# Another written engine order for the units of a gated linear attention in front of a mixture of experts

## The chip, the cores and the metric

The kernel runs on one core of a Trainium2 chip. A core has five engines that run their own instruction streams and meet only at semaphores: PE (TensorE, matmuls into PSUM), DVE (VectorE), ACT (ScalarE), POOL (GpSimd) and SP (which here only issues DMAs). The metric is the device time of one execution in microseconds (us); less is better. A difference of 2% (8 us) is about what a comparison of such runs is taken to show.

## The reference

Two stages follow each other. The first is a recurrent attention over 768 time steps for 4 batches and 8 heads of width 40, the second sends each of the 3072 tokens (rows of 320 numbers) through one of 16 experts.

```
m_new  = max(f[t] + m, i[t])
f_stab = exp(f[t] + m - m_new);  i_stab = exp(i[t] - m_new);  m = m_new
C = f_stab * C + i_stab * outer(v[t], k[t]);   n = f_stab * n + i_stab * k[t]
y[t] = sigmoid(o[t]) * (C @ q[t]) / max(|n . q[t]|, 1)
# x = y as 3072 rows of 320
group  = argmax(x @ w_group);  expert = argmax(x @ w_expert[group])
out[row] = softmax weight of group * softmax weight of expert
           * (relu(x[row] @ w1[expert]) @ w2[expert])
```

## The kernel before, in words

**Units.** The recurrence is cut into chunks of 128 steps. One *unit* is one chunk of one batch with its 8 heads; there are 6 x 4 = 24 units, u = 0 to 23, with chunk c = u // 4 and batch b = u % 4. A unit needs, in the order of the data:

- `decays(u, half)`: for four heads, four matmuls that spread a row of gate sums `Z` over the partitions (L186, into a PSUM tile `sp`), and four exponentials on ACT (L188) into the decay tile `ab`. `upper` (L166, POOL) then zeroes the future half of `ab`.
- `scores(u)` (L197): eight matmuls of keys and queries, 40 rows deep in a 64-row tile, into two more `sp` tiles; `masked` (L202, DVE) multiplies them with `ab` into `pt`.
- `keyw` (L209, POOL) weighs the keys, `state` (L248, PE) makes the new part of the carried matrix, `decayed` (L255, POOL) and `state2` (L266, or L268 in the first chunk, DVE) bring the carried matrix `Cflat` up to date.
- `carried` (L228, PE) multiplies the queries with the carried matrix, `carried2` (L238, DVE) scales the result in PSUM, and `values` (L277, PE) adds `pt` times the values to it.
- `norm1`, `norm2`, `gated` (L283 to L293, DVE), `rows` (L298, POOL) make the finished rows x; `gate` (L163, ACT) is the tanh of the output gate. `store_rows` copies a piece (L305, ACT) and sends x to DRAM; `turn_rows` transposes x (L316, PE) and copies it to SBUF (L318, L319, ACT).

**Routing.** After each chunk `logits` (L341, PE) and the generator `route` (some 18 short DVE steps, one group of small matmuls L385 to L397, one exponential L366) find each token's expert and its place in that expert's list. The steps are "chores", taken a few at a time by `go_on(n)`. `mark` (DVE L472 and L475, POOL L483) and `listing` (L490, PE) build the lists, `listed` (L496, DVE) adds them up. In unit 21 `select` and `load_x` gather the first expert's rows by two indirect DMAs issued by POOL (L593).

**Gates.** `gate_sums` (scans and subtractions on DVE), `parts` (splits the sums into three bf16 rows of `Z`, ACT and DVE in turn), `gate_ends`, `gate_cols` and `gate_scales` make what decays and carried need. Chunk 0 comes first, chunk 1 next, and chunks 2 to 5 together as 512-wide operations.

**What sets the order.** All of this stands under a manual schedule: each engine runs its instructions in the order in which the code calls the stages. Units 1 to 21 come from `unit(u)`, which mixes stages of units u-1, u, u+1 and u+2; units 22 and 23 from `last_units`. The PSUM tiles `sp` are three buffers in turn, and a unit takes four of them. `STEPS` says how many routing steps are taken at the three places of a unit. The experts behind it (L679 to L878) are not touched.

Of the kernel before, what the change touches and what calls it, by code (L numbers as in the profile page):

```python
# [66 lines left out]
def lstm_moe(ctx: ExitStack, tc: tile.TileContext, gates, qkT, nat, wcat, w1, w2, cst, out):  # L67
# [284 lines left out]
    def route(c, bank, lv):  # L352
# [595 lines left out]
    def unit(u):  # L948
        one, two, three = STEPS.get(u) or ((2, 2, 1), (0, 0, 0), (2, 2, 2), (2, 2, 2))[u % B]
        run(load_qk, u + 3)  # L950
        norm1(u - 1)
# [12 lines left out]
        if u + 2 < NU:
            decays(u + 2, 0)
        scores(u + 1)
        if u == NU - 3:
            cast()
        if u % B == 1 and u > B:
            logits()  # L970
        decayed(u)
        if u == 2:
            turn_rows(0)
        rows(u - 1)
        values(u)
        if u + 2 < NU:
            decays(u + 2, 1)
        run(state2, u)
        go_on(two)
        if u == NU - 3:  # L980
            rt["early"] = select(top[:, 0, :], nc.vector)
            xgs[0] = load_x(EARLY, rt["early"], True)
        masked(u + 1, 0)
        masked(u + 1, 1)
        if u == NU - 3:
            do(lows, 1)
        store_rows(u - 1)
        if u == 6:
            first_rows()
        if u > 1:  # L990
            run(keyw, u + 1)
        if u + 2 < NU:
            upper(st_[u + 2]["ab"], 0.0)
        gate(u + 1)
# [427 lines left out]
```

## Time and profile before

| | us |
|---|---|
| median of 3 runs | 399.84 (395.16 to 401.24) |
| profiled execution, its own time | 399.05 |
| its span, first to last instruction | 397.5 |
| PE busy | 363.9 (92%) |
| DVE busy | 315.0 (79%) |
| ACT busy | 255.5 (64%) |
| POOL busy | 158.2 (40%) |

The units take the first 155 us or so, the experts the rest. Among the experts PE is busy nearly all the time; among the units it is not, and the granted clock falls below full in the slices between 20 and 60 us. A unit is recognised in the trace by its group of 16 score matmul records (L197; a matmul of 32-bit numbers leaves two records); the times of these groups are used below as unit marks: scores of unit 2 run from 20.11 us, of unit 6 from 51.75, of unit 7 from 58.63, of 11 from 79.93, of 15 from 101.28, of 19 from 123.41, of 20 from 130.44, of 22 from 140.83 and of 23 from 145.57.

### The profile page before, as it was taken

The numbers are of one execution on the slowest core, as the hardware profiler recorded it, in microseconds if no ns is written. First come the engines' busy times: TensorE is split into PE (matmuls) and PEld (weight loads), VectorE is DVE, ScalarE is ACT, GpSimd is POOL, SyncE is SP. The second block draws the span as 40 slices with busy tenths as digits, with TensorE's granted clock in tenths as the row PEclk, the third lists the DMA queues.
The fourth block names the chain that finished last, engine by engine and source line by source line (L and its number), as shares of the span: only waits on it lengthen the run. The fifth ranks groups of instructions, "written<-read, shape, count | busy, mean of one in ns | idle before, by whom it ended". The sixth has DMA issues, their size and how long they took to land.

```text
span 397.5 us, 10540 instructions
## 1 busy us (share of the span) xinstructions
PE 363.9 (92%) x3993; PEld 331.0 (83%) x3993; DVE 315.0 (79%) x787; ACT 255.5 (64%) x624; POOL 158.2 (40%) x186
## 2 busy tenths in 40 slices
PE   8578598989897998899999999999999999999994
PEld 5467477777776776778999999999999998999993
DVE  3778548888899988547889879878979879899892
ACT  3556545657674674364578566758768768788792
POOL 6266316767755560041532262152243124242221
PEclk9969679999999999899999999999999999999999
DMA  7645326686655699025976585774975786579100
GB/s 202 208 132 170 116 70 188 210 286 193 186 194 156 207 365 350 12 69 189 350 248 255 199 335 181 280 266 157 318 283 181 257 330 222 203 267 327 36 16 16
DMA packets 18886, 81.79 MB, mean 206 GB/s; under 512 B 3248, under 2 KB 7062, under 8 KB 15250
## 3 DMA queue, kind: packets, MB, share of 16 engines
q1 hardware_dynamic: 15010, 68.35, 50.7%
q0 software_dynamic: 3600, 12.39, 8.7%
q8 instruction: 32, 0.52, 0.6%
q10 hardware_dynamic: 224, 0.36, 0.4%
q14 instruction: 20, 0.16, 0.1%
HBM read 71.65 MB, written 9.93 MB: 205 GB/s over the span
## 4 chain that ended last, share of the span: by engine, by line
PE 51%; DVE 15%; issue 15%; POOL 9%; ACT 5%; DMA 2%; POOLq 1%; SPq 0%; ACTq 0%; DVEq 0%
PE psh L767 18%; PE po L817 5%; PE po L819 4%; PE po L818 4%; PE po L695 3%; DVE pt L202 2%; PE acc L277 2%; POOL x L298 2%; PE sp L197 2%; POOL ab L166 2%; POOL kw L209 2%; PE psh L792 2%; PE po L823 1%; POOL out_dram L597 1%; DVE w2l L738 1%
## 5 line engine op out<-in xcount | busy, mean ns | idle before, releaser
L597 POOL DMA_INDIRECT out_dram<-y,ix x32 | 36.8, 1150 | 113.3 <-ACT y L831 85.0
L188 ACT ACTIVATE ab<-sp,bcol 128x128 f32<-128x128 f32 x176 | 50.1, 368 | 27.6 <-PE sp L186 19.7
L767 PE MATMUL psh<-xhl,w1h 128*128 128x256 f32 (+4 forms) x336 | 57.9, 303 | 0.2
L817 PE MATMUL po<-w2h,hh 128*128 128x320 f32 (+1 forms) x176 | 55.6, 316 | 0.0
L819 PE MATMUL po<-w2h,hh 128*128 128x320 f32 (+1 forms) x176 | 54.3, 309 | 0.0
L818 PE MATMUL po<-w2l,hh 128*128 128x320 f32 (+1 forms) x176 | 54.3, 309 | 0.0
L738 DVE TENSOR_TENSOR w2l<-w2s,w2h 128x640 fp32r<-128x640 f32 x60 | 47.8, 823 | 6.4 <-ACT w2h L734 5.7
L767 PEld LDWEIGHTS psh<-xhl,w1h 128*128 128x128 f32 x336 | 49.3, 188 | 2.1 <-DVE xhl L800 0.6
L767 PE MATMUL psh<-xhl,wsk 128*128 128x256 f32 (+4 forms) x168 | 47.5, 322 | 0.0
L767 PE MATMUL psh<-xhl,w1l 128*128 128x128 f32 (+6 forms) x256 | 47.5, 267 | 0.0
L593 POOL DMA_INDIRECT xg<-x_d,ix x32 | 35.8, 1117 | 27.3 <-PE psh L792 7.8
L166 POOL TENSOR_SCALAR_AFFINE_SELECT ab<-ab 128x1024 f32<-128x1024 f32 (+1 forms) x26 | 27.0, 1037 | 48.8 <-ACT ab L188 45.4
L738 DVE TENSOR_TENSOR w1l<-w1s,w1h 128x1024 fp32r<-128x1024 f32 x32 | 39.1, 1222 | 4.2 <-ACT w1h L734 3.9
L767 PEld LDWEIGHTS psh<-xhl,w1l 128*128 128x128 f32 x256 | 42.1, 188 | 0.4
L734 ACT CAST w2h<-w2s 128x640 fp32r<-128x640 f32 x60 | 41.5, 725 | 0.0
L277 PE MATMUL acc<-nt,pt 128*64 128x64 f32 x768 | 30.1, 236 | 6.5 <-DVE acc L238 6.1
L277 PEld LDWEIGHTS acc<-nt,pt 128*64 128x64 f32 x768 | 26.7, 149 | 10.9 <-DVE acc L238 8.3
L734 ACT CAST w1h<-w1s 128x1024 fp32r<-128x1024 f32 x32 | 33.4, 1045 | 0.0
L817 PEld LDWEIGHTS po<-w2h,hh 128*128 128x128 f32 (+1 forms) x176 | 32.6, 185 | 0.3
L819 PEld LDWEIGHTS po<-w2h,hh 128*128 128x128 f32 (+1 forms) x176 | 32.6, 185 | 0.2 <-DVE hh L869 0.2
L818 PEld LDWEIGHTS po<-w2l,hh 128*128 128x128 f32 (+1 forms) x176 | 32.6, 185 | 0.0
L202 DVE TENSOR_TENSOR pt<-sp,ab 128x512 f32<-128x512 f32 x48 | 30.8, 682 | 1.8 <-PE sp L197 1.3
(207 smaller groups left out, 810.6 us busy)
## 6 DMA issues: line engine op xcount, KB each, us to landing
w1s<-in_w_dram SPq DMA_DIRECT2D x12, 1536.0 KB
w2s<-in_w_dram SPq DMA_DIRECT2D x14, 1280.0 KB
nt<-in_nat_dram SPq DMA_DIRECT2D x24, 484.0 KB
qk<-in_qkT_dram SPq DMA_DIRECT2D x48, 160.0 KB
x_d<-x SPq DMA_DIRECT2D x24, 192.0 KB
w1s<-in_w_dram SPq DMA_DIRECT2D x4, 768.0 KB
w1s<-in_w_dram POOLq DMA_DIRECT2D x2, 1536.0 KB, 8.5
w2s<-in_w_dram SPq DMA_DIRECT2D x4, 640.0 KB
```

The lines of the kernel that those rows point to most:

```text
L166: nc.gpsimd.affine_select(out=a, in_=a, pattern=[[0, a.shape[1]], [1, P]], compare_op=ALU.is_ge, fill=fill, base=0, channel_multiplier=-1)
L188: nc.scalar.activation(ab[:, 4 * hh + pr, :], t[:, pr, :], AF.Exp, bias=bcol[:, c, at[pr]:at[pr] + 1])
L202: nc.vector.tensor_tensor(pt, t["pm"][hh], t["ab"][:, 4 * hh:4 * hh + 4, :], op=ALU.mult)
L277: mm(acc[r, j, :], t["pm"][j % 2][:, j // 2, r], nt[:, j * D1:j * D1 + WIN], start=(c == 0 and n == 0), stop=(n == H - 1), skip_group_chec ...
L593: return nc.gpsimd.indirect_dma_start(out=o, out_offset=None, in_=src, in_offset=bass.IndirectOffsetOnAxis(ap=idx, axis=0))
L597: return nc.gpsimd.indirect_dma_start(out=out, out_offset=bass.IndirectOffsetOnAxis(ap=idx, axis=0), in_=y, in_offset=None, bounds_check=N ...
L734: nc.scalar.copy(t[names[0]][:, dst], src[r][:, s])
L738: nc.vector.tensor_tensor(o, src[r][rows, s], h.bitcast(F32), op=ALU.subtract)
L767: mm(ps[:, g, 0:n_], w[:, s], x, start=(part == 0 and n == 0), stop=(part == 1 and n == len(todo[1]) - 1), skip_group_check=True)
L817: mm(po[0:m], hh[:, f, t], w2h[:, s], start=st0, stop=False)
L818: mm(po[0:m], hh[:, f, t], w2l[:, s], start=False, stop=False)
L819: mm(po[0:m], hh[:, f, tl], w2h[:, s], start=False, stop=sp0)
```

## The change

Nothing is computed differently but for the shape of the score matmuls and the place of three small routing results. What moves:

- In `unit(u)` the order becomes: first half of `decays(u+2)`, `carried2(u)`, `decayed(u)`, `scores(u+1)`, the norms of u-1, second half of `decays(u+2)`, `state2(u)`, `keyw(u+1)`, `rows(u-1)`, `values(u)`, `masked(u+1)`, lists, logits, routing steps, `store_rows` and `turn_rows` of u-1, `gate(u+1)`, `state(u+1)`, `carried(u+1)`, `upper(u+2)`, and last the gate steps and marks. Routing steps now stand in one place behind the masks, with a second number for units 18 to 20.
- Unit 0 is now a call of `unit` too. The separate products `spread` for units 0 and 1 (L1182) are gone: these units use `decays` as the others do, which needs `parts(0, P)` first. The rest of the gate work is cut into steps that stand at the ends of units 0 to 5.
- `scores` splits each matmul in two halves of 64 columns: 16 matmuls in 64x64 tiles, four different tiles in turn, for 8 in 64x128.
- Of the routing, `m2` and `oh5` go to PSUM, and one copy (`ohg`) is added per chunk.
- `gate_cols` takes its PSUM tile from the `sp` buffers.

```
 def scores(u):
-                mm(t["pm"][hh][:, pr, :], qk[r, 0, pr, :], qk[r, 1, pr, :], start=True, stop=True)
+                for o in HALVES:
+                    mm(t["pm"][hh][o, pr, :], qk[r, 0, pr, o], qk[r, 1, pr, :], start=True, stop=True, skip_group_check=True)
...
-        m2 = post.tile([P, n * 5], F32, name="m2")
+        m2 = bank[:, LT - P + n * 26:LT - P + n * 31]
...
-        oh5 = post.tile([P, n, 5, 4], F32, name="oh5")
+        oh5 = bank[:, LT + P:LT + P + n * 20].rearrange("p (b g e) -> p b g e", b=n, g=5)
...
+        ohg = post.tile([P, n, 4], F32, name="ohg")
+        nc.vector.tensor_copy(ohg, oh5[:, :, 0, :])
...
+    STEPS = {18: (6, 3), 19: (9, 0), 20: (0, 0)}
...
     def unit(u):
+        n = STEPS.get(u) or ((5, 0), (0, 0), (6, 0), (7, 0))[u % B]
         run(load_qk, u + 3)
+        if u + 2 < NU:
+            decays(u + 2, 0)
+        carried2(u)
+        decayed(u)
+        scores(u + 1)
+        if u:
+            norm1(u - 1)
+            norm2(u - 1)
+            gated(u - 1)
         run(load_nt, u + 3)
+        if u == NU - 3:
+            listed()
+            rt["early"] = select(top[:, 0, :], nc.vector)
+            xgs[0] = load_x(EARLY, rt["early"], True)
+        if u + 2 < NU:
+            decays(u + 2, 1)
+        if u == NU - 3:
+            cast()
+        run(state2, u)
+        keyw(u + 1)
+        if u:
+            rows(u - 1)
+        values(u)
+        masked(u + 1, 0)
+        masked(u + 1, 1)
+        listed()
...
+        if u % B == 1 and u > B:
+            logits()
+        go_on(n[0])
+        if u:
+            store_rows(u - 1)
+            turn_rows(u - 1)
+        gate(u + 1)
+        run(state, u + 1)
+        carried(u + 1)
+        if u + 2 < NU:
+            upper(st_[u + 2]["ab"], 0.0)
+        for x in gate_steps.pop(u, ()):
+            x()
+        go_on(n[1])
+        if u % B == 1 and u > B:
+            chores.append(turned_logits(u // B - 1))
+        if u % B in (1, 3) and B < u < NU - 4:
+            mark()
         if u == NU - 4:
+            listed()
             mark()
             mark()
             fill_up()
+            listing(ps_1.tile([P, 4, P], F32, name="tp", tag="tp"))
...
     def last_units():
         c, d = NU - 2, NU - 1
+        carried2(c)
+        scores(d)
         norm1(c - 1)
         norm2(c - 1)
         gated(c - 1)
-        carried2(c)
-        scores(d)
...
     def parts(lo, hi):
+        nc.scalar.copy(Z[0:n, lo:hi], a)
+        yield
         nc.vector.tensor_tensor(r, a, Z[0:n, lo:hi], op=ALU.subtract)
         yield
+        nc.scalar.copy(m, r)
         nc.scalar.copy(Z[n:2 * n, lo:hi], m)
+        yield
         nc.vector.tensor_tensor(r, r, m, op=ALU.subtract)
         yield
+        nc.scalar.copy(Z[2 * n:3 * n, lo:hi], r)
         yield
...
     def gate_cols(cl, ch):
-        tp = ps_1.tile([P, 8, 64], F32, name="tp", tag="tp" if ch < NCH else "lg")
+        tp = ps_s.tile([P, 8, 64], F32, name="tp", tag="sp")
...
-        steps(first, 5)
+        steps(first, 4)
+        early = parts(0, P)
+        steps(early)
+        steps(first)
+        gate_cols(0, 1)
+        steps(early, 4)
...
-        spread(0, 0)
-        spread(0, 1)
+        decays(0, 0)
         scores(0)
+        decays(0, 1)
...
+        decays(1, 0)
+        steps(early, 2)
         masked(0, 1)
+        state(0)
+        decays(1, 1)
+        steps(early, 3)
...
+        far2 = parts(2 * P, S)
+        one, two = (lambda: steps(far)), (lambda: steps(far2))
+        gate_steps.update({0: [near_scales, one], 1: [lambda: gate_ends(1, 2), one, one], 2: [one], 3: [one, two],
+                           4: [two, two], 5: [two, two, far_scales]})
+        for u in range(6):
             unit(u)
```

On PE, in one unit of the steady stretch (u = 9; `sp` is the decay or score tile, `st` the new state, `acc` the output, `tp` the transposed rows, each L186 pair stands four times), the order before, from the first decay half of unit 11 on:

```order
L186 LDWEIGHTS ind_b
L186 MATMUL sp<-Z,ind_b 128x128
...
L197 MATMUL sp<-qk_107 128x128 x8
L341 MATMUL lg<-xT,wc 32x128 x12
L277 MATMUL acc<-nt_114,pt 64x64 x16
L186 LDWEIGHTS ind_b
L186 MATMUL sp<-Z,ind_b 128x128
...
L248 MATMUL st<-nt_115,kw 40x41 x8
L228 MATMUL acc<-Cflat,qk_107 64x2x41 x8
L347 MATMUL lg<-cs,lgT 128x128
```

The same unit with the change:

```order
L186 LDWEIGHTS ind_b
L186 MATMUL sp<-Z,ind_b 128x128
...
L198 MATMUL sp<-qk_107 64x128 x16
L186 LDWEIGHTS ind_b
L186 MATMUL sp<-Z,ind_b 128x128
...
L278 MATMUL acc<-nt_114,pt 64x64 x16
L342 MATMUL lg<-xT,wc 32x128 x12
L317 MATMUL tp<-cs,x 128x128 x2
L317 MATMUL tp<-cs,x 64x128
L249 MATMUL st<-nt_115,kw 40x41 x8
L229 MATMUL acc<-Cflat,qk_107 64x2x41 x8
L348 MATMUL lg<-cs,lgT 128x128
```

The second decay half moved from behind the values to right behind the scores, and the transposes of the rows from the unit's end to right behind the values.

On POOL, from unit 19 to unit 21 (`x` are finished rows, `ab` the masked decays, `mark` the list products, `xg` the gathered rows), the order before:

```order
L166 AFFINE_SELECT ab_110<-ab_110 128x1024
L483 TENSOR_TENSOR mark<-mark,iw 128x2x48 x4
L298 TENSOR_TENSOR x<-sr,den 128x320
L166 AFFINE_SELECT ab_111<-ab_111 128x1024
L298 TENSOR_TENSOR x<-sr,den 128x320
L593 DMA xg<-x_d,ix 128x384 x2
L166 AFFINE_SELECT ab_112<-ab_112 128x1024
```

And with the change:

```order
L166 AFFINE_SELECT ab_110<-ab_110 128x1024
L485 TENSOR_TENSOR mark<-mark,iw 128x2x48 x2
L299 TENSOR_TENSOR x<-sr,den 128x320
L166 AFFINE_SELECT ab_111<-ab_111 128x1024
L485 TENSOR_TENSOR mark<-mark,iw 128x2x48 x4
L595 DMA xg<-x_d,ix 128x384 x2
L299 TENSOR_TENSOR x<-sr,den 128x320
L166 AFFINE_SELECT ab_112<-ab_112 128x1024
```

The four mark products of unit 20 now stand behind the rows and the mask of that unit, and the rows of unit 20 behind the two gathers.

## Rows read from the trace of the kernel before

**Rows 1.** Busy time by stretch: start:end, length, then PE, PEld, DVE, ACT, POOL, granted clock

```profile
20.11:51.75 31.64, 23.45 (x340) 19.76 (x341) 21.36 (x46) 17.10 (x59) 16.15 (x17) 0.72 0.48 147
51.75:58.63 6.88, 6.88 (x117) 5.47 (x116) 3.70 (x15) 3.25 (x13) 0.51 (x1) 0.73 0.01 2
58.63:79.93 21.30, 19.00 (x407) 16.35 (x405) 17.49 (x62) 13.52 (x51) 15.32 (x26) 1.00 0.66 202
79.93:101.28 21.35, 19.41 (x410) 16.77 (x408) 18.51 (x64) 13.63 (x51) 13.99 (x21) 1.00 0.72 224
101.28:123.41 22.13, 19.42 (x410) 16.77 (x409) 19.93 (x69) 13.50 (x51) 13.97 (x21) 1.00 0.60 186
```

**Rows 2.** Waits by engine and line, 60 to 165 us: total us, times, longest

```profile
PE lg L385 <- DVE oh L380: 5.1, 5, 1.7
PE acc L277 <- DVE acc L238: 3.3, 4, 1.8
PE st L248 <- POOL kw L209: 2.7, 5, 1.5
```

**Rows 3.** Timeline of PE in one unit: start, us, operation, records, [idle before]

```profile
90.34 0.39 PE L186 MATMUL sp<-Z,ind_b 96*128 96x128 bf16 x4
90.66 1.16 PE L197 MATMUL sp<-qk 64*128 64x128 f32 x16
91.75 1.15 PE L277 MATMUL acc<-nt,pt 128*64 128x64 f32 x32
92.83 0.40 PE L186 MATMUL sp<-Z,ind_b 96*128 96x128 bf16 x4
93.55 0.51 PE L248 MATMUL st<-nt,kw 128*40 128x41 f32 x16 [0.32 <-POOL kw L209]
```

**Rows 4.** Timeline of PE and ACT: a decay half and its exponentials on an idle ACT

```profile
88.60 0.40 PE L186 MATMUL sp<-Z,ind_b 96*128 96x128 bf16 x4
...
89.10 1.14 ACT L188 ACTIVATE ab<-sp,bcol 128x128 f32<-128x128 f32 x4 [1.08 <-PE sp L186]
```

**Rows 5.** Timeline of PE: 128-column matmuls in one tile, and in four tiles in turn

```profile
5.41 1.15 PE L1182 MATMUL wide<-A__129,cs 32*128 32x128 f32 x8
...
96.37 1.00 PE L341 MATMUL lg<-xT,wc 128*32 128x128 f32 x24
```

**Rows 6.** Timeline, 42 to 52 us: PE at the lower clock, the last gate chain

```profile
42.91 1.98 PE L277 MATMUL acc<-nt,pt 128*64 128x64 f32 x32 [2.87 <-DVE acc L238]
...
48.68 0.61 ACT L1116 CAST Z<-Dl 32x512 bf16<-32x512 f32 x1
...
51.75 2.08 PE L197 MATMUL sp<-qk 64*128 64x128 f32 x16
51.86 1.15 ACT L188 ACTIVATE ab<-sp,bcol 128x128 f32<-128x128 f32 x4
```

**Rows 7.** A DVE group in one cycle, 79.93 to 101.28 us: busy us, mean ns | idle

```profile
L266 DVE TENSOR_TENSOR Cflat<-Cflat,st 40x164 f32<-40x164 f32 x8 | 2.6, 324 | 1.9 <-POOL Cflat L255 1.8
```

**Rows 8.** Busy time by stretch: units 19 and 20, unit 21, and what follows

```profile
130.44:140.83 10.39, 9.36 (x160) 7.99 (x158) 9.93 (x39) 6.53 (x25) 5.64 (x10) 1.00 0.78 255
140.83:145.57 4.74, 4.74 (x99) 3.76 (x97) 4.21 (x13) 3.91 (x14) 3.13 (x3) 1.00 1.02 318
145.57:154.47 8.90, 7.27 (x132) 6.43 (x131) 7.76 (x19) 5.79 (x16) 2.63 (x4) 1.00 0.94 342
```

**Rows 9.** Timeline of POOL and DVE: marks of unit 20, index and gathers of unit 21, rows

```profile
137.14 1.39 POOL L483 TENSOR_TENSOR mark<-mark,iw 128x96 f32<-128x96 f32 x4 [1.34 <-DVE mark L475]
...
142.35 0.16 DVE L512 COPY ix<-lsum 128x3 f32<-128x3 f32 x1
...
142.74 1.18 POOL L593 DMA_INDIRECT xg<-x_d,ix  x1 [1.30 <-DVE ix L512]
...
144.21 1.47 POOL L593 DMA_INDIRECT xg<-x_d,ix  x1 [0.30 <-issue]
```

More of the change, by code (lines that the diff above doesn't have):

```diff
@@ L336, in logits @@
     def logits():
-        bank = rt["bank"] = ps_1.tile([P, LT + P], F32, name="lg")
+        bank = rt["bank"] = ps_1.tile([P, 512], F32, name="lg")
         for k in range(3):
@@ L408, in route @@
         sg = post.tile([P, n, 4], F32, name="sg")
-        nc.vector.tensor_tensor(sg, s5[:, :, 1:5], ohg, op=ALU.mult)
+        nc.vector.tensor_tensor(sg, s5[:, :, 1:5], oh5[:, :, 0, :], op=ALU.mult)
         yield "on"
@@ L948, in unit @@
     def unit(u):
-        one, two, three = STEPS.get(u) or ((2, 2, 1), (0, 0, 0), (2, 2, 2), (2, 2, 2))[u % B]
+        n = STEPS.get(u) or ((5, 0), (0, 0), (6, 0), (7, 0))[u % B]
         run(load_qk, u + 3)
-        norm1(u - 1)
-        norm2(u - 1)
-        gated(u - 1)
-        run(load_nt, u + 3)
+        if u + 2 < NU:
[7 more added lines that the diff above has]
+            gated(u - 1)
+        run(load_nt, u + 3)
+        if u == NU - 3:
[14 more added lines that the diff above has]
+        listed()
         if u == 9:
             last_rows()
-        go_on(one)
-        run(carried2, u)
-        listed()
+        if u == NU - 3:
+            do(lows, 1)
+        if u == 6:
+            first_rows()
+        if u % B == 1 and u > B:
[16 more added lines that the diff above has]
+            mark()
         if u == NU - 4:
+            listed()
             mark()
@@ L963, in unit @@
             fill_up()
[L964 to L994, printed above, removed]
-        run(state, u + 1)
-        go_on(three)
-        run(carried, u + 1)
-        if u % B == 1 and u > B:
-            chores.append(turned_logits(u // B - 1))
-        if u % B == 2 and u > B:
-            go_on(1)
-        if u > 1:
-            turn_rows(u - 1)
-        if u % B < 2 and B < u < NU - 4:
-            mark()
+            listing(ps_1.tile([P, 4, P], F32, name="tp", tag="tp"))
         if u == min(ASIDE):
@@ L1137, in gate_scales @@
         nc.scalar.activation(eacol[:, cl:ch, :], tp[:, cl:ch, 32:64], AF.Exp)
-    def later_gates(rest):
-        for _ in parts(P, 2 * P, nc.scalar.copy):
-            yield
-        gate_ends(1, 2)
-        for _ in range(4):
-            next(rest)
-            yield
-        for _ in parts(2 * P, S, nc.scalar.copy):
-            yield
-        gate_ends(2, NCH - 1)
-        gate_scales(gate_cols(2, NCH), 2, NCH)
-        yield
     with tc.manual_schedule():
@@ L1191, in lstm_moe @@
-        spread(0, 0)
-        spread(0, 1)
+        steps(first, 4)
[4 more added lines that the diff above has]
+        steps(early, 4)
+        load_nt(2)
+        decays(0, 0)
         scores(0)
+        decays(0, 1)
+        upper(st_[0]["ab"][:, 0:4], 0.0)
+        upper(st_[0]["ab"][:, 4:8], 0.0)
         keyw(0)
-        early = parts(0, P, nc.scalar.copy)
-        steps(early)
+        steps(near, 4)
+        early = parts(P, 2 * P)
@@ L1197, in lstm_moe @@
         masked(0, 0)
-        spread(1, 0)
-        spread(1, 1)
-        keyw(1)
+        steps(near)
+        decays(1, 0)
+        steps(early, 2)
         masked(0, 1)
-        steps(early)
-        scores(1)
+        state(0)
+        decays(1, 1)
+        steps(early, 3)
         gate(0)
-        gate(1)
-        state(0)
-        steps(early)
-        masked(1, 0)
-        values(0)
-        masked(1, 1)
-        state2(0)
-        steps(near, 5)
-        tp = gate_cols(1, 2)
-        state(1)
@@ L1215, in lstm_moe, with near_scales, far_scales @@
-        gate_scales(tp, 1, 2)
-        decays(2, 0)
-        decays(2, 1)
-        keyw(2)
-        upper(st_[2]["ab"], 0.0)
-        steps(far)
-        nc.sync.dma_start(wc, wcat)
-        chores.append(later_gates(far))
-        for u in range(1, 6):
+        upper(st_[1]["ab"], 0.0)
+        nc.sync.dma_start(wc, wcat)
+        def near_scales():
+            gate_scales(gate_cols(1, 2), 1, 2)
+        def far_scales():
+            gate_ends(2, NCH - 1)
+            gate_scales(gate_cols(2, NCH), 2, NCH)
```

26 lines of the change are left out of this document (3 added, 23 removed).

## The prediction, made before the changed kernel was run

> **What bounds the kernel now.** I read the busy time by stretch first [rows 1]. From the scores of unit 7 on, a cycle of four units takes 21.30, 21.35 and 22.13 us with PE busy for 19.00, 19.41 and 19.42 of them: PE is close to the bound there, and a new order can give back at most the 2 to 3 us of its idle time in each cycle. DVE follows with 17.49 to 19.93 us. The first units are different: from the scores of unit 2 to those of unit 7 (five units, 38.5 us) PE is busy for 23.45 + 6.88 us, at a granted clock of 0.72 and 0.73, that is, a mixture of the full level (2.4 GHz) and the half one (1.2 GHz). The waits say who is late in the steady part [rows 2]: the routing's `oh` (5.1 us in five waits), `carried2` (3.3 us) and `keyw` (2.7 us), each a result of another engine that comes just before PE needs it. After unit 23 the experts keep PE busy; neither their code nor their order changes, so the change is worth what it does before 154.5 us [rows 8].
>
> **The sum is made against the profiled execution's own time, 399.05 us** (0.8 us below the median, 399.84; the three runs spread over 6 us). A comparison of this kernel can tell about 2%, 8 us, from no change.
>
> **1. The prologue: 0.** Removed are the `spread` products (1.15 us for eight [rows 5]) and their exponentials; added are the `parts` of chunk 0 in front of the first decays. These are four ACT copies and two DVE subtractions in turn, for which I take 2.4 us (an estimate: six operations at 0.4 us, somewhat below the 0.61 us of the four times wider copy [rows 6]). The first spread starts at 5.41 us [rows 5], so the first decays come at about 7.7. Up to the scores of unit 2, six decay halves follow each other through ACT: 1.75 us each, 0.50 us from the first product to the first exponential (88.60 to 89.10 [rows 4]), 1.14 us of exponentials and 0.1 us to the next. With some 1.7 us of other ACT work these scores come at about 20 us, as now (20.11). From nothing hidden to all hidden this is +2 to -2 us.
>
> **2. Units 2 to 6: -8.8.** Now they take 38.5 us, because gate steps and PE's work stand in each other's way: the values wait 2.87 us, then run for 1.98 us at the lower clock against 1.15 later, and the scores 2.08 against 1.16 [rows 3, 6]. In the new order a gate step stands at a unit's end, behind all that PE needs next. DVE has 21.36 + 3.70 = 25.1 us of work in the five units [rows 1], so they can't take less than that. I take five units at 4.5 us (22.5: the PE time of part 3 without its lists and logits), two of them at the lower clock (each (1.98 - 1.15) + (2.08 - 1.16) = 1.75, so 3.5), and the last gate chain, which stays: from the last copy to `Z` to the first exponentials behind it 48.68 to 51.86, 3.2 us [rows 6], so 3.4 with its first steps. That is 29.4 us, 9.1 less than 38.5; I take 8.8, for scores 0.3 later at unit 2. Bounds: all at the lower clock gives five times 1.75 for 3.5, 5.3 us worse (-3.5); none, and the chain hidden behind the units' work, gives 25.1 by DVE (-13.4).
>
> The Trainium skill, "TensorE: Matmul & The Clock Gate", section "HAM oscillation — how this bites in real kernels", describes an engine that falls back to half clock after its idle gaps and pays again at each restart. By it a new order that only trades one gap for another could leave the whole stretch at the lower level; the trace agrees as far as that its lower clock stands where PE idles most [rows 1].
>
> **3. Steady cycles, units 7 to 18: -2.** The products of a unit are a decay half 0.32 us, scores 1.09, values 1.08 (start to start [rows 3]). What is removed: carried is asked for half a unit earlier than it is needed, `keyw` and `rows` stand ahead of the masks, and the routing stands behind them in one piece, so the three waits of [rows 2] (11.1 us over the whole) should go. What is added: the second decay half now stands right behind the scores. Of three `sp` buffers the first half has one and the scores two, so it needs the one that the exponentials of the first half release: 0.50 + 1.14 + 0.06 = 1.70 us after the first half began. PE gets there after 0.32 + 1.09 = 1.41 us: a wait of 0.29 us in each unit, 1.16 in a cycle. Behind it stand the values.
>
> The scores' own price is not in the trace: 32 records in four 64x64 tiles for 16 in two. Lower bound 1.00 us for 24 records in four tiles in turn [rows 5], so 40 ns each and 1.3 us; upper bound, if only two tiles run at a time, twice the present 1.09, 2.18. I take 1.3, since the four-tile row is nearest. Up to 1.70 - 0.32 = 1.38 us it costs nothing: the wait hides it.
>
> The floor of a cycle is then PE's busy time + 1.16: 20.2, 20.6 and 20.6 us. To it I add 0.5 for the one unit in four in which the routing's exponential on ACT stands behind DVE's masks and steps, and the copies of x, the tanh and the next unit's exponentials behind it. Against 21.30, 21.35 and 22.13 the gains are 0.6, 0.25 and 1.0: about -2. In the third cycle DVE's 19.93 us leave little room under 21.1. Bounds: 0 (the wait doubles, all else right) and -5 (no wait, no ACT delay). The results that go to PSUM, the copy `ohg`, and where `state2` stands (324 ns each time [rows 7]) move DVE by tenths of a microsecond in a cycle in which PE is the bound: 0.
>
> **4. Units 19 and 20: +2.0.** They take 10.39 us now, DVE busy for 9.93 [rows 8], so nothing can be gained from a new order of DVE. All the routing steps and marks of the last chunk but one are still to be done there, and in the new order the list products (`listing`, PE) stand at unit 20's end, ahead of what unit 21 needs, and wait for POOL's last products of `mark`: four in 1.39 us now, which wait 1.34 for DVE [rows 9]. As PE waits in order, I take 1.4 + 0.6 for the rest of that chain: +2.0; bounds 0 and +3.
>
> **5. From unit 21 on: +2.8.** POOL issues the two gathers from 142.74 to 145.68, 2.9 us, behind the index at 142.35 [rows 9]. They now stand ahead of the rows of unit 20, and PE's transposes of these rows, in unit 21, ahead of state and carried. The gathers can begin about 2 us into unit 21 and last 2.9, the rows 0.6, a hop to PE 0.4: about 6 us, against the 4.0 or so at which PE reaches these transposes: +1.9. `last_units` adds `norm` and `gated` behind `carried2` of unit 22: +0.9, since from there DVE is busy for 7.76 of 8.90 us [rows 8]. Bounds: 0, if the index is early; +4.
>
> **The sum:** 0 - 8.8 - 2 + 2.0 + 2.8 = -6.0, so **393.0 us**.
>
> **The rivals.**
>
> *The new order does all it can* (386 us). Units 2 to 6 at full clock (3.5 less), half of the tail's losses (2.4 less), a cycle more (1 less). For it: DVE has slack in the first units, and PE's long wait [rows 6] is for one result that the order moves. Against it: the last gate chain is serial over three engines.
>
> *The gain is eaten* (399 us). The early units give 4 only because DVE is nearly as busy there as PE, the cycles nothing, since the new wait replaces those removed, and the tail costs 4.8: +0.8 without the prologue, some 399 with a little from it. For it: DVE at 9.93 of 10.39 us [rows 8], and waits that in a tight cycle move rather than vanish.
>
> *Only two score tiles run at a time* (411 us, slower). The scores then last 2.18 us, and the second decay half begins 0.32 + 2.18 - 1.70 = 0.80 us later in each of some 22 units: 17.6 us on 393. Against it: the four-tile row with 40 ns a record [rows 5]. It decides against the kernel before from 2.0 us of scores on (0.65 us each in 22 units is 14 us, to 407).
>
> *ACT is late* (413 us, slower). ACT is busy for 13.5 us of a cycle [rows 1], 3.4 in a unit of 5.3; in the new order it alternates between PE, DVE and POOL. If the exponentials of the first half start 1.0 us later than the 0.50 [rows 4], because the copies of x before them wait for PE's late transposes, the second half is later by as much in some 20 units. It decides from 0.7 us on.
>
> *The clock falls in the steady units too* (414 us). Rule or not, the mechanism is that a wait of 0.29 us in each unit takes the full clock away, and twelve units pay 1.75 us each: 21 us. Against it: now the same units idle 2 us in a cycle at a granted clock of 1.00 [rows 1]. [...]
>
> **How the numbers follow.** The forecast (389 to 397 as its own range) has 0.47, the fuller gain 0.25, the eaten gain 0.15, two tiles at a time 0.05, ACT late 0.05, the lower clock 0.03. Below 391.8 us (2% under 399.84) lie nearly all of the fuller gain and a quarter of the forecast: 0.37. Over 407.8 lie the three slow cases: 0.13. The rest, 0.50, is within 2%. For 8 in 10 the range takes in most of the fuller gain (from 384) and the eaten one (to 403).
>
> **What would show it.** Right, if the scores of unit 7 start near 49.8 us with fewer microseconds below full clock before it; if PE's waits for `oh`, `carried2` and `keyw` are gone and one of 0.3 us for the exponentials ahead of the second decay half stands in each unit; if the scores last 1.1 to 1.4 us; if PE waits at the end of unit 20 for the marks and in unit 21 for the rows behind the gathers. Wrong, if the scores of unit 7 start after 55 us, if the wait behind the scores is over 0.7 us, or if the tail from unit 19 on is not longer than now.

## The result, and the profile after the change

The changed kernel takes 394.75 us (median of 20 runs, 392.93 to 396.50) against 399.65 (20 runs of the kernel before): a ratio of 0.990, 95% interval 0.987 to 0.992. It is faster by 1.0%, which is within the 2% that the forecast called no change; the forecast was 393.0 us with a range of 384 to 403. The profiled execution took 394.56 us with a span of 393.0, so 4.5 us less than before by their spans.

Where these 4.5 us are shows in the busy time between unit marks (starts of a unit's scores, L198 after the change): first units 0 to 4, 4 to 8, 8 to 19, 19 to 22 and 22 to 23, before (columns as in [rows 1]; the last two are the busy share of the DMA engines and GB/s):

```profile
7.56:32.98 25.42, 19.11 (x278) 16.30 (x277) 17.96 (x42) 14.44 (x55) 10.04 (x12) 0.80 0.55 168
32.98:65.08 32.10, 24.05 (x412) 20.06 (x410) 19.94 (x52) 17.03 (x60) 16.57 (x25) 0.79 0.46 141
65.08:123.41 58.33, 53.18 (x1120) 45.79 (x1119) 51.50 (x178) 37.31 (x138) 37.37 (x53) 1.00 0.65 202
123.41:140.83 17.42, 14.59 (x266) 12.59 (x264) 16.24 (x64) 9.98 (x38) 9.89 (x17) 1.00 0.68 218
```

and the same marks after:

```profile
8.09:31.07 22.98, 17.86 (x339) 14.45 (x337) 14.75 (x35) 15.38 (x56) 10.69 (x13) 0.78 0.58 172
31.07:55.28 24.21, 21.02 (x464) 17.16 (x462) 18.68 (x53) 16.99 (x57) 15.00 (x23) 0.93 0.61 193
55.28:113.52 58.24, 53.81 (x1303) 44.87 (x1301) 52.57 (x187) 39.01 (x137) 38.96 (x55) 1.00 0.66 209
113.52:133.05 19.53, 15.45 (x318) 13.15 (x316) 16.44 (x64) 10.66 (x37) 9.27 (x15) 0.97 0.78 251
133.05:138.86 5.81, 5.81 (x113) 4.50 (x113) 3.24 (x7) 4.42 (x14) 3.93 (x4) 0.81 0.71 259
```

The start costs 0.5 us, units 0 to 4 gain 2.4, units 4 to 8 gain 7.9 (with a granted clock of 0.93 instead of 0.79), the eleven units from 8 to 19 gain 0.1, units 19 to 22 lose 2.1, unit 22 loses 1.1 (4.74 in [rows 8]; its scores now last 1.99 us instead of 1.10, as at the half clock), and what follows loses 2.2. Four of the waits of PE over the whole span, after (total us, times, longest), and the one left for `carried2`:

```profile
PE sp L186 <- ACT ab L188: 8.2, 21, 1.2
PE lg L387 <- DVE oh L382: 4.0, 3, 1.9
PE tp L317 <- DVE lists L498: 2.1, 3, 1.0
PE tp L492 <- DVE fill L552: 1.7, 1, 1.7
PE acc L278 <- DVE acc L239: 0.3, 1, 0.3
```

The waits of [rows 2] for `carried2` and `keyw` are gone from the steady part but for one of 0.3 us (a wait of 1.3 us for `kw` lies in the prologue), and that for `oh` stands only in units 18 and later. In their place stands the wait for `ab` ahead of the second decay half: 11 times from unit 7 to 19, 2.9 us in all, the longest 0.54. In one unit:

```profile
60.10 1.10 PE L198 MATMUL sp<-qk 64*64 64x128 f32 x32
61.46 0.38 PE L186 MATMUL sp<-Z,ind_b 96*128 96x128 bf16 x4 [0.26 <-ACT ab L188]
```

### The profile page after: what moved, and what is told of

The parts are those of the page before. It is cut to its first block, busy times and chain, and to the rows that moved or that the text cites. A ratio compares the mean times of both kernels' runs of the same rounds, so it can differ in the third digit from the quotient of the medians.

```text
span 393.0 us, 11283 instructions
## 1 busy us (share of the span) xinstructions
PE 361.9 (92%) x4361; PEld 326.1 (83%) x4361; DVE 313.5 (80%) x793; ACT 258.8 (66%) x624; POOL 156.0 (40%) x185
## 4 chain that ended last, share of the span: by engine, by line
PE 47%; issue 8%; DVE 7%; ACT 2%; POOL 2%; POOLq 1%; DVEq 0%; ACTq 0%
PE psh L769 19%; PE po L819 5%; PE po L820 5%; PE po L821 5%; PE po L697 3%; PE psh L794 2%; PE po L825 2%; PE po L824 1%; DVE w1l L740 1%; POOL out_dram L599 1%; PE tp L492 1%; PE psh L681 1%; DVE w2l L740 1%; POOLq L843 1%; ACT w1h L736 1%
## 5 line engine op out<-in xcount | busy, mean ns | idle before, releaser
L188 ACT ACTIVATE ab<-sp,bcol 128x128 f32<-128x128 f32 x192 | 54.8, 368 | 25.4 <-PE sp L186 18.4
L595 POOL DMA_INDIRECT xg<-x_d,ix x32 | 33.3, 1040 | 28.3 <-PE psh L794 7.7
L166 POOL TENSOR_SCALAR_AFFINE_SELECT ab<-ab 128x1024 f32<-128x1024 f32 (+1 forms) x25 | 26.5, 1061 | 24.1 <-ACT ab L188 24.1
L198 PE MATMUL sp<-qk 64*64 64x128 f32 x768 | 29.9, 292 | 0.2 <-ACT ab L188 0.2
L769 PEld LDWEIGHTS psh<-xhl,wsk 128*128 128x128 f32 x168 | 29.5, 189 | 0.2
```

Of the source, the lines that this page charges most:

```text
L166: nc.gpsimd.affine_select(out=a, in_=a, pattern=[[0, a.shape[1]], [1, P]], compare_op=ALU.is_ge, fill=fill, base=0, channel_multiplier=-1)
L188: nc.scalar.activation(ab[:, 4 * hh + pr, :], t[:, pr, :], AF.Exp, bias=bcol[:, c, at[pr]:at[pr] + 1])
L198: mm(t["pm"][hh][o, pr, :], qk[r, 0, pr, o], qk[r, 1, pr, :], start=True, stop=True, skip_group_check=True)
L595: return nc.gpsimd.indirect_dma_start(out=o, out_offset=None, in_=src, in_offset=bass.IndirectOffsetOnAxis(ap=idx, axis=0))
L769: mm(ps[:, g, 0:n_], w[:, s], x, start=(part == 0 and n == 0), stop=(part == 1 and n == len(todo[1]) - 1), skip_group_check=True)
```

## The experiments

The ratios are against the kernel before, run beside each experiment at 399.1 to 399.4 us. The profiles are of one execution each.

**The shape of the score matmuls** (`e1_tiles128`):

```diff
-                for o in HALVES:
-                    mm(t["pm"][hh][o, pr, :], qk[r, 0, pr, o], qk[r, 1, pr, :], start=True, stop=True, skip_group_check=True)
+                mm(t["pm"][hh][:, pr, :], qk[r, 0, pr, :], qk[r, 1, pr, :], start=True, stop=True)
```

> The changed kernel with the score matmuls back in 64x128 tiles (eight instead of sixteen). The forecast held that the shape is worth nothing as long as the scores end before the exponentials of the first decay half do: 394.7 us as the changed kernel (within 1.5), the group of score records 1.16 us long instead of 1.10, the wait ahead of the second decay half 0.06 shorter, 0.2 instead of 0.26. A rival: the 64x64 shape saves the switch of tile shape between scores and values, and without it each unit pays some 0.1 to 0.2 us: 397 to 399.

394.35 us, ratio 0.986 (0.982 to 0.990): as the changed kernel. The scores last 1.16 us instead of 1.10, and the wait behind them is that much shorter, 0.20 instead of 0.26:

```profile
60.81 1.16 PE L197 MATMUL sp<-qk 64*128 64x128 f32 x16
62.17 0.38 PE L186 MATMUL sp<-Z,ind_b 96*128 96x128 bf16 x4 [0.20 <-ACT ab L188]
```

The shape changes nothing in the time. The changed kernel's 1.10 us are far from the 2.18 that the forecast worked out for two tiles at a time.

**The wait of the second decay half** (`e2_half_behind`): `decays(u + 2, 1)` goes from behind the norms to behind `values(u)`.

```diff
-        if u + 2 < NU:
-            decays(u + 2, 1)
...
         values(u)
+        if u + 2 < NU:
+            decays(u + 2, 1)
         masked(u + 1, 0)
```

> The changed kernel with the second decay half back behind the values. Theory A (step 3 of the forecast: the wait of 0.2 to 0.5 us ahead of the second half in each of some 20 units is lost time): that wait goes, the cycles from unit 7 to 19 get 2 to 3 us shorter over all, 392 us. Rival B (the wait moves): the second exponentials start about 1 us later in each unit, behind them ACT's copies, and POOL's mask, so that the next scores or keyw wait as long; the cycles stay within 0.5 of 64.3 us, 395 us.

395.19 us, ratio 0.985 (0.979 to 0.991; one of its four runs took 391.51). Units 7 to 19 take 65.4 us instead of 64.3. PE's waits there, in the changed kernel 2.9 us for `ab` and 1.4 for others, are now 5.5; the largest two:

```profile
PE tp L317 <- DVE lg L402: 2.2, 2, 1.2
PE acc L278 <- DVE acc L239: 1.7, 2, 1.1
```

Rival B holds: the wait is taken away and DVE is late instead. DVE is busy for 18 to 21 us of a cycle of 21 to 22 in the changed kernel, and the wait of 0.25 us in each unit was not time that could be had back.

**Gate steps in front, in the new order** (`e3_gates_front`):

```diff
             decays(u + 2, 0)
+        for x in gate_steps.pop(u - 1, ()):
+            x()
         carried2(u)
...
-        for x in gate_steps.pop(u, ()):
-            x()
+        if u == 5:
+            for x in gate_steps.pop(u, ()):
+                x()
```

> The changed kernel with the gate steps of units 0 to 4 put at the front of the next unit, behind its first decay half and ahead of carried2 and the norms, so that DVE does them before what PE waits for. Theory A (step 2 of the forecast: the early units gained because the gate steps stand behind all that PE needs next): PE waits again for carried2 or the new state, about 1 us in each of units 2 to 5, and the clock falls again; scores of unit 2 to those of unit 7 take 31 to 34 us instead of 27.0, 399 to 402 us. Rival B (it is the order of the stages as a whole): 27 to 28.5 us, 395 to 396.

395.31 us, ratio 0.988 (0.983 to 0.992). Units 0 to 4 and 4 to 8, in the slowest of its four runs (396.39):

```profile
7.94:33.31 25.37, 21.32 (x338) 17.06 (x338) 15.72 (x36) 14.91 (x56) 10.26 (x12) 0.60 0.51 162
33.31:54.84 21.53, 19.44 (x464) 15.90 (x462) 17.86 (x47) 16.34 (x57) 14.90 (x24) 1.00 0.61 191
```

2.4 us are lost in the first stretch, where the granted clock is 0.60 instead of 0.78, and 2.7 won in the second, where it now stays full; scores of unit 2 to 7 take 27.5 us from their first record, 26.5 from where the group runs on. In the new order the place of the gate steps decides nothing over all.

**Gate steps at the end, in the old order** (`e4_before_gates_end`, the kernel before with its table changed, and with the PSUM tile of the last gate columns taken from `sp` as in the change):

```diff
-    STEPS = {1: (2, 0, 1), 2: (2, 0, 0), 3: (2, 0, 0), 4: (2, 0, 0), 5: (3, 0, 0), ...
+    STEPS = {1: (0, 0, 3), 2: (0, 0, 2), 3: (0, 0, 2), 4: (0, 0, 2), 5: (0, 0, 3), ...
...
-        tp = ps_1.tile([P, 8, 64], F32, name="tp", tag="tp" if ch < NCH else "lg")
+        pool, tag = (ps_1, "tp") if ch < NCH else (ps_s, "sp")
+        tp = pool.tile([P, 8, 64], F32, name="tp", tag=tag)
```

> The kernel before with one part of the change alone: in units 1 to 5 all gate steps are taken at the third place, behind the state at the unit's end, instead of ahead of carried2 (and the last gate columns take their PSUM tile from the decay tiles, as in the change). Theory A (the place of the gate steps makes the gain): scores of unit 2 to those of unit 7 fall from 38.5 us to 30 to 33, 392 to 395 us. Rival B (the order of the stages as a whole): they fall by 2 us at most, 398 to 400.

398.02 us, ratio 0.995 (0.992 to 0.997). From unit 2 to 7 it takes 36.0 us, measured as the 38.5 before (from the larger part of unit 2's group, 21.82): 2.5 less, near rival B. By the two stretches it is neither:

```profile
8.68:37.26 28.58, 20.29 (x279) 17.36 (x278) 16.54 (x43) 15.01 (x57) 10.33 (x14) 0.76 0.46 142
37.26:63.88 26.62, 21.22 (x411) 18.11 (x409) 18.41 (x52) 16.37 (x57) 14.12 (x22) 0.94 0.49 151
```

Units 4 to 8 gain 5.5 us of the 7.9, units 0 to 4 lose 3.2: the split of chunk 1 now ends just ahead of unit 4's decays, and PE waits 2.8 us for `Z`. The changed kernel does that split in the prologue.

**The same with the steps cut to one engine each** (`e9_before_gates_cut`): `parts` with a yield after each engine's piece, as in the change, in the rhythm (0, 0, 5), (0, 0, 2), (0, 0, 3), (0, 0, 2), (0, 0, 3); the PSUM tile as in e4.

```diff
+        nc.scalar.copy(Z[0:n, lo:hi], a)
+        yield
         nc.vector.tensor_tensor(r, a, Z[0:n, lo:hi], op=ALU.subtract)
         yield
```

> The kernel before with the gate work of units 1 to 5 cut as in the change: each step holds the work of one engine (a copy on ACT or a subtraction on DVE), the steps stand at the unit's end in the rhythm of the changed kernel, and no unit before the fifth holds a round trip from ACT to DVE and back. The order of the other stages stays that of before. Theory C (the early gain comes from cutting the round trips into one-engine steps): scores of unit 2 to those of unit 7 fall from 38.5 us to 29 to 32, 392 to 395 us. Theory B (it is the order of the stages): they stay above 35, 397 to 399.

402.52 us, ratio 1.009 (1.005 to 1.012), slower by 0.9%. My rhythm left the last resume of the gate steps over, so that the routing behind it runs one step late; from unit 6 on it is no clean comparison. And its first number leaves all five pieces of chunk 1's split in unit 1, so that one round trip stays whole. The early stretches:

```profile
7.74:35.70 27.96, 19.58 (x279) 16.62 (x278) 16.53 (x43) 15.00 (x57) 10.30 (x14) 0.82 0.53 155
35.70:64.42 28.72, 22.69 (x412) 19.16 (x410) 17.56 (x49) 16.42 (x58) 14.70 (x23) 0.88 0.49 155
```

From unit 2 to 7 it takes 36.2 us, above 35, as theory B has it. Cutting on top of moving gives no more than moving alone, and unit 1's split is exposed again (PE waits 2.9 us for `Z`). Theory C is not borne out, as far as so unclean a run can tell.

**Moved, but not in unit 1** (`e10_before_later_gates_end`, the PSUM tile as in e4):

```diff
-    STEPS = {1: (2, 0, 1), 2: (2, 0, 0), 3: (2, 0, 0), 4: (2, 0, 0), 5: (3, 0, 0), ...
+    STEPS = {1: (2, 0, 1), 2: (0, 0, 2), 3: (0, 0, 2), 4: (0, 0, 2), 5: (0, 0, 3), ...
```

> The kernel before with the gate steps of units 2 to 5 alone at the third place, behind the state (as e4_before_gates_end); those of unit 1, the split of chunk 1's sums, stay where they were. In e4 the scores of unit 4 to those of unit 8 fell from 32.1 to 26.6 us, while those of unit 0 to unit 4 grew from 25.4 to 28.6 because the split of chunk 1 was exposed at the end of unit 1. Theory A (the place of the gate steps is worth most of the early gain, as step 2 of the forecast says, where nothing else is exposed): 25 to 26 us up to unit 4, 26 to 27 from there to unit 8, 393.5 to 395.5 us. Theory B (only the order of all stages gives it): the time lost in e4 comes back elsewhere, 397 to 399.

394.72 us, ratio 0.989 (0.983 to 0.996): one line of a table in the old order, with that PSUM tile, brings as much as the whole change, as far as these intervals can tell. What the tile alone is worth was not tried. The stretches of its profile (which is its slowest run, 396.58), both longer than theory A had them (25 to 26 and 26 to 27):

```profile
7.62:33.93 26.31, 19.20 (x278) 16.31 (x278) 17.52 (x43) 15.06 (x57) 10.32 (x14) 0.81 0.52 163
33.93:61.96 28.03, 22.63 (x412) 19.20 (x410) 18.41 (x52) 16.27 (x57) 14.08 (x22) 0.88 0.45 143
```

So 4.1 of the 7.9 us of units 4 to 8 come from the place, and units 0 to 4 lose 0.9. What was in the way in the old order is a round trip: copy on ACT, subtraction on DVE, copies, subtraction, all ahead of `carried2`, for which PE waited 2.87 us and then ran at the half clock [rows 6]. With the round trip moved behind, a shorter wait is left, now behind DVE's gate sums, and the values run in 1.15 us instead of 1.98:

```profile
41.03 1.15 PE L277 MATMUL acc<-nt,pt 128*64 128x64 f32 x32 [1.71 <-DVE acc L238]
```

In e3, where the steps stand in front but each holds one engine's work, PE does not wait for `carried2` there at all. The other 3.8 us I did not isolate; 3.6 of them lie between the scores of units 6 and 7 (12.0 us here, 8.5 in the changed kernel), where both kernels have the last gate chain.

**The lists ahead of the masks, and unit 0 from separate products** (`e5_listed_spread`):

```diff
+        listed()
         masked(u + 1, 0)
         masked(u + 1, 1)
-        listed()
...
+                mm(wide[h][:, k % 4, :], bc(ident[0:32, k:k + 1], (32, P)), A_[:, 0:P], start=True, stop=True)
...
-        decays(0, 0)
         scores(0)
-        decays(0, 1)
```

> The changed kernel with two edits far apart. (1) The adding up of the lists on DVE stands ahead of the two masks instead of behind them; it is what frees the PSUM tile of the transposes. If PE's waits for the lists ahead of the transposes (2.1 us in three: units 15, 17 and 19) are lost time, they go and units 17 and 19 are 0.9 shorter each; if DVE is the bound there, another wait takes their place and the scores of unit 15 to those of unit 20 stay at 27.7 us. (2) The decays of unit 0 come from separate products of the 32-bit gate sums again, as before the change, while the three-part split runs behind the first exponentials. If the prologue's loss (scores of unit 2 at 22.2 us instead of 20.1) is the split that stands ahead of the first decays, they come at about 21; if it is the chain of decay halves through ACT, at 22. Together 392 to 393 us in the one case, 394 to 395 in the other.

393.21 us, ratio 0.986 (0.980 to 0.992). The scores of unit 2 come at 20.82 instead of 22.21: 1.4 us of the prologue's loss was the split ahead of the first decays. The third cycle, units 15 to 19, gains 1.0 (22.14 in the changed kernel):

```profile
89.99:111.10 21.11, 19.67 (x474) 16.46 (x472) 19.63 (x74) 14.27 (x50) 13.77 (x20) 1.00 0.58 194
```

PE's wait for the lists is gone there. From the scores of unit 19 to those of 20 it loses 0.9 us (6.44 for 5.55), so that from unit 15 to 20 the rival holds, 27.6 us for 27.7. The next unit wins 1.0 and the one behind it loses 0.8 (9.48 for 8.69). At the scores of unit 23 this kernel is 1.55 us ahead of the changed one, 1.4 of them from the prologue: alone, the lists' new place is worth 0.2 us at most.

**The gathers behind the rows** (`e6_gathers_behind`):

```diff
-            xgs[0] = load_x(EARLY, rt["early"], True)
...
             rows(u - 1)
+        if u == NU - 3:
+            xgs[0] = load_x(EARLY, rt["early"], True)
         values(u)
```

> The changed kernel with the two indirect gathers of unit 21 behind the rows of unit 20 on POOL. Step 5 of the forecast: the gathers hold up the rows and with them PE's transposes by 1.9 us; then unit 21 is 1 to 2 us shorter, 393 us. The trace of the changed kernel shows no wait of PE ahead of these transposes; if that is right, the move is worth 0 to 0.3 us, or costs up to 1 as the gathered rows come later: 394.5 to 395.5.

393.96 us, ratio 0.987 (0.981 to 0.993), and the same span, 393.0. The rows move from 136.60 to 133.11, and PE reaches their transposes at the same time, without a wait in either:

```profile
137.50 0.55 PE L317 MATMUL tp<-cs,x 128*128 128x128 f32 x3
```

**The list products of unit 20 behind the scores of unit 21** (`e7_listing_later`):

```diff
         scores(u + 1)
+        if u == NU - 3:
+            listing(ps_1.tile([P, 4, P], F32, name="tp", tag="tp"))
...
-            listing(ps_1.tile([P, 4, P], F32, name="tp", tag="tp"))
```

> The changed kernel with the list products of unit 20's end put behind the scores of unit 21 on PE, so that decays and scores need not wait for the marks. Step 4 of the forecast: PE's wait (1.7 us) and the fall of the clock behind it (list products, decays and scores at the half clock, about 1.9 us) go, 2 to 3 us shorter up to the scores of unit 22, less what the later index and gathers cost at the end: 392 to 394 us. Rival: DVE, with index and selection behind the products, moves the wait into unit 21: 394.5 to 395.5.

395.45 us, ratio 0.989 (0.986 to 0.992): the rival. The wait of 1.7 us and the half clock behind it go, and PE waits for the rows, which now do stand behind late gathers:

```profile
129.95 1.10 PE L198 MATMUL sp<-qk 64*64 64x128 f32 x32
131.35 1.30 PE L492 MATMUL tp<-mark 128*128 128x96 f32 x8 [0.30 <-POOL mark L485]
...
138.21 0.55 PE L317 MATMUL tp<-cs,x 128*128 128x128 f32 x3 [3.32 <-POOL x L299]
```

**e5, e6 and e7 together** (`e11_combined`): in addition, ACT's copies of the gate work stand in the middle of units, the last three pieces of chunk 1's split in units 0 and 1 instead of the prologue, and unit 0's state behind the second decay half of unit 1:

```diff
+        gate_steps.update({0: [near_scales, one, three], 1: [one, one], 2: [lambda: gate_ends(1, 2), one], 3: [two],
+                           4: [two], 5: [far_scales], 6: [lambda: gate_ends(2, NCH - 1)]})
+        mid_steps.update({0: [three], 1: [three], 3: [two], 4: [two], 5: [two, one]})
```

> The changed kernel with the edits that paid and the two of unit 20 and 21 together: lists added up ahead of the masks; unit 0's decays from separate products; chunk 1's split and the last chunks' split cut so that ACT's copies stand in the middle of units 0, 1, 3, 4 and 5 and DVE's subtractions at their ends; the last gate columns at unit 5's end, the last gate ends at unit 6's; the list products of unit 20 behind the scores of unit 21 and the gathers behind the rows. If the wait ahead of unit 8's decays (scores of unit 6 to 7: 8.5 us, and the clock falling behind it) is the last gate chain, these 8.5 become 5 to 6 us. If e7's wait came from the gathers ahead of the rows, unit 20 to 22 get 2 us shorter. Together 386 to 389 us; if the waits only move, 391 to 393.

389.43 us, ratio 0.979 (0.972 to 0.985), between the two forecasts. Scores of unit 6 to 7 take 6.8 us instead of 8.5, but by the scores of unit 9 that is lost again (19.6 us from unit 6 for 19.3). Its 6.0 us of span are gained in the prologue (2.4), from unit 15 to 19 (1.0) and most of all from unit 19 to 22, which is 2.5 us shorter than in the changed kernel. There the list products are late as in e7, but with the rows ahead of the gathers as in e6 PE does not wait for rows behind them:

```profile
110.44:127.42 16.98, 13.76 (x310) 11.64 (x308) 13.97 (x57) 10.36 (x37) 8.35 (x12) 1.00 0.70 229
132.29 0.55 PE L317 MATMUL tp<-cs,x 128*128 128x128 f32 x3
```

e6 and e7 were not run together without the other edits.

**Matmuls that compute nothing** (`e11b_busy`, on top of e11):

```diff
         scores(0)
+        busy(5, ps_a, "it")
...
         decays(1, 0)
+        busy(2, ps_a, "it")
         decays(1, 1)
```

> The kernel e11_combined with seven matmuls that compute nothing used (128x512 bf16) in the two stretches of the prologue in which PE waits for the exponentials, so that PE does not idle there. If PE's idle time between 8.6 and 13 us is what makes the clock fall to the half level from 13 to 21 us, the scores and values of units 1 and 0 take 1.1 instead of 2.0 us each and the scores of unit 2 come 1 to 2 us earlier than in e11_combined; if ACT's chain sets that stretch anyway, they come at the same time.

387.78 us, ratio 0.974 (0.968 to 0.981), an interval that overlaps with that of e11. The 4 us in which PE waits and the 8 behind them, in the changed kernel:

```profile
9.00:13.00 4.00, 1.31 (x26) 0.92 (x20) 1.40 (x5) 2.78 (x11) 2.13 (x3) 0.92 0.89 242
13.00:21.00 8.00, 6.63 (x102) 5.46 (x98) 3.62 (x7) 4.89 (x17) 2.63 (x3) 0.50 0.57 178
```

in e11_combined:

```profile
9.00:13.00 4.00, 1.37 (x24) 0.94 (x18) 3.80 (x9) 2.82 (x11) 1.71 (x3) 0.90 0.90 248
13.00:21.00 8.00, 7.48 (x142) 6.40 (x138) 4.36 (x7) 5.86 (x22) 3.65 (x4) 0.62 0.46 161
```

and in e11b_busy:

```profile
9.00:13.00 4.00, 2.51 (x31) 1.40 (x29) 3.29 (x8) 3.03 (x12) 1.40 (x2) 1.00 0.91 257
13.00:21.00 8.00, 6.60 (x162) 5.41 (x161) 6.88 (x15) 6.52 (x25) 5.07 (x5) 1.00 0.45 162
```

The last number but two is the granted clock: 0.50, 0.62, 1.00. The scores of unit 2 come at 17.21 us, 2.6 earlier than in e11 (19.84). The kernel e12 below has the same prologue and the same fillers, and in its execution the clock fell all the same, for a shorter time; its scores of unit 2 come at 18.26:

```profile
13.00:21.00 8.00, 7.85 (x162) 6.65 (x161) 5.86 (x14) 6.03 (x23) 3.96 (x5) 0.79 0.36 140
```

Without fillers these 8 us run at 0.50 in the changed kernel and in each of e1, e2, e3, e5, e6 and e7, and at 0.62 in e11. So the fillers raise the clock, and by how much differs from one execution to the next.

**The gate ends earlier in unit 6** (`e12_ends_mid`):

```diff
-                           4: [two], 5: [far_scales], 6: [lambda: gate_ends(2, NCH - 1)]})
+                           4: [two], 5: [far_scales]})
```

with the step in `mid_steps` of unit 6 instead.

> The kernel e11b_busy with the last gate ends in the middle of unit 6, right behind the masks, instead of at its end, where DVE has the routing steps ahead of them and PE waits 1.8 us. If that wait is lost time, it goes: the scores of unit 7 to those of unit 8 take 4.8 to 5.2 us instead of 6.6, and the kernel 386.0 to 386.5 us; if DVE is behind in that unit anyway, another wait of 1 us or more takes its place and the time stays at 387.5.

387.51 us, ratio 0.973 (0.968 to 0.978): no different from e11b. The rival: DVE reaches the step only behind the masks at 47.5 us, PE comes earlier and waits 1.6 us, and the clock falls behind it. From the scores of unit 7 to those of 8 it takes 8.2 us instead of 6.6.

```profile
48.05 0.20 PE L1134 MATMUL tp<-ends,ones_b 96*128 96x96 bf16 x1 [1.62 <-DVE ends L1132]
...
50.05 1.34 PE L229 MATMUL acc<-Cflat,qk 128*64 128x82 f32 x16
```

Both are faster than the kernel before by some 2.6%, and than the changed one by some 1.7%.

## Why the prediction was right, point by point

The time was 1.75 us from the forecast, and the sum of its terms -6.0 against -4.5 in the spans. The terms themselves were less good, and that their errors cancel (-2.7 and -1.5 against +2.1, +1.5, +1.6 and +0.5) is in part luck:

| term | predicted | measured |
|---|---|---|
| 1. scores of unit 2 | 0 | +2.1 (22.21 for 20.11) |
| 2. scores of unit 2 to 7 | -8.8 | -11.5 (27.0 us) |
| 3. 7 to 19 | -2 | -0.5 (64.3 for 64.8) |
| no term: 19 to 20 | none | -1.5 (5.55 for 7.03) |
| 4. 20 to 22 | +2.0 | +3.6 (13.98 for 10.39) |
| 5. from scores of unit 22 | +2.8 | +3.3 |

**1, mis-sized.** The split of chunk 0 was sized rightly: the first decays come at 7.78 us for the 7.7 worked out. What failed is the step "six decay halves follow each other through ACT: 1.75 us each". The exponentials of the six start at 8.20, 9.81, 11.43, 14.01, 17.18 and 18.98 us. Ahead of the fourth PE waits 1.3 us for `keyw`, and ahead of the fifth ACT does the copies of chunk 1's split, which the change puts there:

```profile
14.01 1.14 ACT L188 ACTIVATE ab<-sp,bcol 128x128 f32<-128x128 f32 x4 [1.28 <-PE sp L186]
...
17.18 1.13 ACT L188 ACTIVATE ab<-sp,bcol 128x128 f32<-128x128 f32 x4
```

Taking chunk 0's split from in front gives 1.4 us back (e5). PE idles meanwhile and then runs at 0.50 of its clock, the level of 1.2 GHz, up to 21 us; in e11's prologue, by e11b and e12, this costs 1.6 to 2.6 us. The Trainium skill, "TensorE: Matmul & The Clock Gate", section "HAM oscillation — how this bites in real kernels", names idle gaps as what brings the half clock; the prologue agrees, 0.62 in e11 against 1.00 in e11b and 0.79 in e12, where the gaps are filled, though no single wait there is longer than 1.4 us.

**2, right mechanism, too small.** Terms 1 and 2 belong together, since the change moves chunk 1's split from the one stretch to the other: -9.4 at the scores of unit 7 (49.23 us against the 49.8 forecast). The term that was too dear is the 3.5 us for two units at the lower clock; there is none:

```profile
22.21:49.23 27.02, 22.77 (x539) 18.53 (x539) 22.30 (x55) 20.04 (x68) 17.58 (x24) 0.99 0.60 192
```

Without it the sum gives 25.9 for the 27.0 measured. (The forecast read from [rows 1] that the lower clock stands where PE idles most; from 51.75 to 58.63 us PE is busy throughout and the clock is 0.73, so it stands behind the idle time too.) That gate steps ahead of what PE needs cost the early units is borne out by e10, but for the PSUM tile that moved with them; that they must stand behind it, as I wrote, is not: e3 has them in front, cut small, and loses nothing over all.

**3, the wait as forecast, the gain not.** The wait is 0.2 to 0.5 us a unit, the scores 1.10 us. The cycles are:

```profile
49.23:70.35 21.12, 20.42 (x467) 16.79 (x465) 18.36 (x63) 14.30 (x51) 12.85 (x18) 0.92 0.60 178
70.35:91.38 21.03, 19.67 (x475) 16.53 (x473) 18.60 (x65) 14.21 (x50) 14.23 (x21) 1.00 0.73 239
91.38:113.52 22.14, 19.78 (x474) 16.53 (x472) 20.59 (x79) 14.16 (x50) 14.21 (x21) 1.00 0.60 188
```

Of the 11.1 us of waits in [rows 2], only 6.6 lie in units 7 to 19; the rest is behind them. In these units PE's waits fall from 6.6 to 4.3 us, but its busy time, which the forecast held fixed, grows from 57.8 to 59.9. The second cycle took 21.03 us for the 21.1 worked out (20.6 + 0.5). In the first (21.12 for 20.7) the clock was at 0.92 behind the last gate chain and PE is busy 1.4 us longer, and in the third (22.14 for 21.1) PE waits 1.1 us for `listed`, which the change puts behind the masks and which I did not cost; e5 takes that wait away, but what it gains is lost again by the scores of unit 22. Of the slower rivals, two tiles at a time would show as scores of 2.18 us (1.10), a late ACT as waits of 0.7 us or more ahead of the second half (at most 0.54 from unit 7 on), and a falling clock as less than the 1.00 from unit 8 to 19.

**Between 3 and 4, a stretch without a term.** The cycles end at the scores of unit 19 and the 10.39 us of term 4 begin at those of unit 20 [rows 8]; the 7.03 us between were put at no change without a reason. They gain 1.5: PE waited 1.8 us for `carried2` there, the longest of that kind in [rows 2], and now waits for nothing longer than 0.25.

**4, right mechanism, too small.** PE waits 1.66 us at the end of unit 20. The profile names `fill` on DVE, but the list products do not read `fill`; they read the products of `mark`, for which their weight load waits 1.83 us, and the first two of these four end at 130.97 us, just ahead of the list products at 131.02:

```profile
130.19 1.39 POOL L485 TENSOR_TENSOR mark<-mark,iw 128x96 f32<-128x96 f32 x4 [1.53 <-DVE mark L477]
```

So the wait is the one forecast. The term left out that the list products behind it take 1.67 us instead of the 1.30 of e7, and that the transposes of the rows wait 0.96 us for the lists in the unit before.

**5, about the right size, the cause in part wrong.** The step "about 6 us, against the 4.0 or so at which PE reaches these transposes" failed: the rows are finished 4.3 us into the unit, since the gathers begin after 1.1 us and not 2, and PE, late and slow from term 4, reaches them at 4.35 us:

```profile
136.60 0.74 POOL L299 TENSOR_TENSOR x<-sr,den 128x320 f32<-128x320 f32 x1
137.40 0.55 PE L317 MATMUL tp<-cs,x 128*128 128x128 f32 x3
```

E6 shows the move to be worth nothing here, and e7 that the wait is there as soon as term 4 does not hide it (3.32 us). What the trace shows instead is unit 22 longer by 1.1 with scores at 1.99 us, and behind unit 23 a wait for `oh` that is 1.2 us longer than before (0.75 in the first line, 1.91 in the second):

```profile
149.13 0.19 PE L385 MATMUL lg<-oh,lt_b 128*128 128x64 bf16 x1 [0.75 <-DVE oh L380]
143.58 0.19 PE L387 MATMUL lg<-oh,lt_b 128*128 128x64 bf16 x1 [1.91 <-DVE oh L382]
```

Whether that is the forecast's second piece, the norms behind `carried2` (+0.9), and where the remaining 1.0 us of the 3.3 go, was not tried.

## What to carry to other kernels

In an order written by hand, look for work that goes from one engine to another and back ahead of something a third waits for. Moving it behind, or handing out one engine's piece at a time, shortened the wait here (e10, e3), unless the moved work then ends just ahead of something else (e4). Two edits that are worth nothing apart may pay together (e6 and e7, in e11), and a wait that is removed shows whether it was lost time only by what takes its place (e2, e5, e12). Add up an order change by unit marks that leave no gap, since terms of both signs, and a stretch without a term, can hide in a total that is right.

## What was not expected of the hardware

Seven 128x512 matmuls that compute nothing, 1.85 us of PE in stretches where it waited, took the granted clock of the 8 us from 13 to 21 us from 0.62 (e11) to 1.00 in one execution (e11b) and to 0.79 in another (e12). Elsewhere a wait of about 0.25 us in each unit of some 5 us left the clock at 1.00 over 58 us.
